# Fused attention and two MLPs in float32: GpSimd's operations in pieces of 128 columns, one-column thresholds, second PSUM banks for h and y, the low parts of k on VectorE

## The chip, the core and the metric

The kernel runs on one core of one Trainium2 chip. The core has a matrix engine (TensorE, PE in the profile), a vector engine (VectorE, DVE), an engine for activation functions (ScalarE, ACT), a programmable engine (GpSimd, POOL in the profile and "Pool" in the kernel) and SyncE (SP), on whose queue all the large DMAs are issued. TensorE writes only to PSUM, a small memory of eight banks per partition; GpSimd works only from SBUF to SBUF. The metric is the device time of one execution in microseconds.

## The reference

All data are float32. A thresholded attention (4 batches, 8 heads, 576 positions, head size 64) feeds an MLP of 512 -> 2048 -> 512 with a SiLU gate, and this a second MLP of 512 -> 1536 -> 512 whose two branches are multiplied.

```
scores = scale * q @ k.T                                  # scale = 1/8
thresh = max(scores) - tau                                # tau = 0.02
scores = where(scores >= thresh, scores, -1e9)
attn = exp(scores - max(scores)); attn /= sum(attn) + 1e-9
x = (attn @ v) as [2304, 512]
h = x @ w_in;  y = (h * sigmoid(h)) @ w_out               # 512 -> 2048 -> 512
a = y @ w_a;  b = y @ w_b;  out = (a * b) @ w_o           # 512 -> 1536 -> 512
```

## The kernel before

A matrix product in float32 is made of three faster products: each operand is split into a high part, rounded to the format fp32r, and a low part, which is the float32 value minus the high one (hi x lo, hi x hi and lo x hi). So every weight, every x, every gated h, every y and z is split by ScalarE (the cast to the high part) and DVE or Pool (the subtraction).

The weights come as pairs of 32-bit words. A block of 128x512 weights passes through `split_weight`: DMA into `wraw`; ScalarE scales the low words (`low`, into `wt`) and the high words (`scale`, into `wc`); DVE masks the sign (`sign`, L323) and joins it to the scaled words (`join`, L328); Pool adds the two (`total`, L332, 128x512); ScalarE casts the high part (`hi`, L336, into `w`); Pool, for some of the second MLP's blocks DVE, subtracts for the low part (`lo`, L340, 128x512). There is one buffer for `wc`, so the next block's `scale` waits for this block's `total`. The first MLP has 32 such blocks, the second 36.

The attention works on 144 tiles of 128 rows by 576 columns. For each, TensorE writes scores to the two-bank PSUM tile `sa` (in the first sixteen tiles, the early ones, in turn `sa` and `sb`); DVE scales them into `t` and finds the lowest (L489); a tiny DVE instruction on 128x1 makes the threshold `thr` (L495 early, L497 later); ScalarE takes the exponential `e` (L503); DVE masks it and sums it (L506, one SBUF input and PSUM in the early tiles, later the two SBUF tensors `t` and `e`); TensorE transposes `e` into `tp`, ScalarE copies that out, and TensorE multiplies with `v`. The sums get 1e-9 added on DVE (`guard`, L435), are inverted, go through DRAM (`r_d`) and come back broadcast as `xi`, Pool multiplies with them (`divide`, L618), and x goes to DRAM as `xT_d`. From tile 54 on q and k are split as well (`split_head`): a cast on ScalarE and two subtractions on Pool (`lo_k`, L402, and `lo_q`, L405, 576 columns each).

The first MLP takes blocks of 256 tokens (j, nine of them) and slices of 128 of the 2048 hidden columns (f, sixteen); a pair (j, f) is a unit, numbered n from 0 to 143. A unit's `mlp1_up` is 12 matmuls into the PSUM bank `hb`; then ScalarE takes the tanh, DVE the gate (`th`, L711, which reads `hb` a last time and so frees it), ScalarE the high part `gh` and DVE the low part `gl` (L717). `mlp1_down` is 12 matmuls into the two-bank tile `sb`, which gathers y over the sixteen units of a token block and is then copied out in two halves by ScalarE and DVE (`yo`, L765); y goes through DRAM (`yT_d`) to the second MLP, whose units write the PSUM pair `ps_a` and `ps_b` (two pairs in turn, opened when attention closes).

The order of instructions on every engine is written ahead of time by a planner, the class `Plan`: each task has an engine, a cost in ns, a rank and the tasks that it waits for; the planner runs through time, gives each idle engine its ready task of lowest rank, and records the program in that order. At run time each engine keeps its order and waits on semaphores. While the attention has gaps on TensorE, units of the first MLP fill them, and in the longest gaps transposes of `ident` into `tp` that nobody reads (filler). A number of the planner concerns us: tasks of DVE and Pool that are marked `port` cannot run at the same time, so whichever comes second is given the remaining time of the other on top:

```
shared = max(0, min(port["Pool" if e == "DVE" else "DVE"] - now, t["cost"]))
port[e] = end = done = end + self.SHARED * shared
```

Of the kernel before, what the change touches and what calls it, by code (L numbers as in the profile page):

```python
# [21 lines left out]
P = 128  # L22
# [38 lines left out]
class Plan:  # L61
# [15 lines left out]

    SHARED = 1.0
# [42 lines left out]
    def run(self):  # L121
# [4 lines left out]
        port = {"DVE": 0, "Pool": 0}  # L126
# [12 lines left out]
        while events:  # L139
# [13 lines left out]
            for e, q in ready.items():  # L153
                if idle[e] and q:
# [41 lines left out]
def pool_ns(n):  # L196
    return int(2.35 * n + 90)
# [7 lines left out]
def fused_kernel(ctx: ExitStack, tc: tile.TileContext, qk, qk2, v, tau, w_in, w_out, w_a, w_b, w_o2, out):  # L205
# [25 lines left out]
    RINGS = dict(qk=2, sp=2, v=1, t=2, e=4, pa=1, pb=1, sa=1, sb=1, tp=2, hb=1, av=1, x=1, xi=1, rs=1,  # L231
# [48 lines left out]

    back = const.tile([P, 1], F32, name="back")
# [16 lines left out]
    def split_weight(key, src, rank, dst, after=(), lo_engine="Pool", scale_engine="DVE"):  # L298
# [32 lines left out]
        def total():  # L331
            nc.gpsimd.tensor_tensor(out=s["t"], in0=s["c"].bitcast(U32), in1=s["t"], op=ALU.add)  # L332
# [5 lines left out]
        def lo():  # L338
            eng = nc.gpsimd if lo_engine == "Pool" else nc.vector
            eng.tensor_tensor(out=wt[key][:, 1, :], in0=s["t"].bitcast(F32), in1=wt[key][:, 0, :].bitcast(F32),  # L340
                              op=ALU.subtract)
# [48 lines left out]
    def split_head(n, b, h):  # L390
# [18 lines left out]
        q, k = (add("Pool", pool_ns(S), n + R_SPLIT, f, [up]) for f in (lo_q, lo_k))  # L409
# [17 lines left out]
    def inverses(n, m):  # L427
# [6 lines left out]
        def guard():  # L434
            nc.vector.tensor_scalar(out=s["sum"][:, :m], in0=s["sum"][:, :m], scalar1=EPS, scalar2=None, op0=ALU.add)  # L435
# [19 lines left out]
    def softmax(parts, total):  # L455
# [69 lines left out]
    def weigh(b, half, c, tiles, v, last):  # L525
# [91 lines left out]
        def divide():  # L617
            nc.gpsimd.tensor_tensor(out=s["x"][:, :nq], in0=s["x"][:, :nq], in1=s["i"][:, :nq], op=ALU.mult)  # L618
# [40 lines left out]
    def load_x(j):  # L659
        s = xs[j] = {}  # L660

        def split(c):
# [12 lines left out]
            def lo():  # L675
                nc.gpsimd.tensor_tensor(out=s["l", c], in0=s["r", c], in1=s["h", c].bitcast(F32), op=ALU.subtract)
# [13 lines left out]

# [305 lines left out]
```

## Time and profile before

| what | us |
|---|---|
| median of 3 runs (1200.87 to 1204.55) | 1202.97 |
| the profiled execution | 1202.49 |
| its span | 1200.7 |
| TensorE busy (97% of the span) | 1162.6 |
| weight loads busy (83%) | 998.2 |
| DVE busy (54%) | 648.1 |
| ScalarE busy (45%) | 544.5 |
| Pool busy (23%) | 278.9 |

The span is from the first to the last instruction of the program, and the profiled execution's own time is 1.8 us more. An engine's busy time is the time in which at least one of its instructions runs; a time spent waiting inside an instruction counts as busy. Matmuls follow each other more closely than they last, so TensorE's busy time is no measure of its work; the number of matmuls in a stretch says more.

### The profile page before, as it was taken

What the parts mean: (1) busy time and instruction counts of PE and PEld (TensorE: products, weight loads), DVE (VectorE), ACT (ScalarE), POOL (GpSimd) and SP (SyncE); (2) the same over time, 40 slices, a digit from 0 to 9 for tenths busy, and PEclk for the clock granted to TensorE, in tenths of its full rate; (3) what the DMA queues carried; (4) which work ended last, traced back from release to release, by engine and by line L of the source; (5) the groups of instructions that cost most, each with busy time, mean ns of one, the idle gap of its engine ahead of it and who ended that gap; (6) DMA issues with size and microseconds to landing.
All of it is one profiled execution on the core that took longest, in us unless ns stands there. A gap on an engine that the chain in (4) does not pass through costs nothing.

```text
span 1200.7 us, 19670 instructions
## 1 busy us (share of the span) xinstructions
PE 1162.6 (97%) x7675; PEld 998.2 (83%) x7675; DVE 648.1 (54%) x1428; ACT 544.5 (45%) x1071; POOL 278.9 (23%) x232
## 2 busy tenths in 40 slices
PE   8889989999999999989999999999999999999998
PEld 5556667888888888889999999888888888888898
DVE  7989898777777777473233258765311211221121
ACT  7777777666666666443233245443211211211121
POOL 3656554233322322130000024443000000000000
PEclk9989999999999999999999999999999999999999
DMA  5655543222322220351010023432200200000000
GB/s 190 195 176 150 160 152 129 80 85 86 97 72 71 89 89 32 101 166 36 1 37 27 1 66 117 152 123 71 70 1 1 70 1 1 18 36 1 1 36 18
DMA packets 43276, 90.14 MB, mean 75 GB/s; under 512 B 4384, under 2 KB 22448, under 8 KB 43184
## 3 DMA queue, kind: packets, MB, share of 16 engines
q1 hardware_dynamic: 43040, 88.89, 23.0%
q8 instruction: 60, 0.98, 0.4%
q14 instruction: 32, 0.26, 0.1%
q10 hardware_dynamic: 144, 0.00, 0.0%
HBM read 74.65 MB, written 14.23 MB: 74 GB/s over the span
## 4 chain that ended last, share of the span: by engine, by line
PE 76%; DVE 10%; DMA 5%; issue 4%; ACT 4%; POOL 1%; SPq 0%; DVEq 0%; ACTq 0%; POOLq 0%
PE op L869 12%; PE ps_b L825 12%; PE ps_a L825 12%; PE hb L699 12%; PE sb L746 12%; PE av L583 5%; PE tp L538 5%; PE sa L473 4%; DVE e L506 3%; DMA xi<-r_d 2%; DVE t L489 1%; DVE wraw L323 1%; DVE thr L497 1%; DVE wc L328 1%; DVE gl L717 1%
## 5 line engine op out<-in xcount | busy, mean ns | idle before, releaser
L699 PE MATMUL hb<-xh,w 128*128 128x256 f32 x1152 | 225.1, 290 | 6.0 <-DVE th L711 3.9
L699 PEld LDWEIGHTS hb<-xh,w 128*128 128x128 f32 x1152 | 179.3, 192 | 14.2 <-DVE th L711 6.2
L746 PE MATMUL sb<-gh,w 128*128 128x256 f32 x1152 | 169.6, 286 | 2.3 <-DVE yo L765 1.8
L699 PE MATMUL hb<-xl,w 128*128 128x256 f32 x576 | 162.9, 283 | 0.0
L835 DVE TENSOR_TENSOR z<-ps_b,z 128x512 f32<-128x512 f32 (+1 forms) x60 | 38.2, 636 | 230.2 <-PE ps_b L825 230.2
L746 PEld LDWEIGHTS sb<-gh,w 128*128 128x128 f32 x1152 | 150.5, 192 | 6.6 <-DVE yo L765 2.8
L506 DVE SCALAR_TENSOR_TENSOR e<-t,thr,e 128x576 f32<-128x576 f32 x128 | 129.7, 1014 | 21.8 <-ACT e L503 20.8
L825 PE MATMUL ps_a<-yh,w 128*128 128x512 f32 (+1 forms) x480 | 137.0, 370 | 0.0
L825 PE MATMUL ps_b<-yh,w 128*128 128x512 f32 (+1 forms) x480 | 136.6, 369 | 0.0
L869 PE MATMUL op<-w,zh 128*128 128x512 f32 x432 | 134.3, 392 | 0.0
L489 DVE TENSOR_SCALAR_CACHE_REDUCE t<-sa,nscale 128x576 f32<-128x576 f32 x128 | 103.6, 809 | 51.6 <-PE sa L473 49.6
L538 PE MATMUL tp<-ident,e 128*128 128x128 f32 x706 | 106.5, 280 | 13.9 <-DVE e L506 10.0
L711 DVE SCALAR_TENSOR_TENSOR th<-th,hb 128x256 f32<-128x256 f32 x144 | 60.2, 418 | 107.2 <-ACT th L708 106.8
L332 POOL TENSOR_TENSOR wt<-wc,wt 128x512 uint32<-128x512 uint32 x68 | 91.2, 1342 | 109.5 <-DVE wc L328 91.3
L503 ACT ACTIVATE e<-t,min 128x576 f32<-128x576 f32 x128 | 99.6, 780 | 28.2 <-DVE t L489 27.5
L708 ACT ACTIVATE th<-hb 128x256 f32<-128x256 f32 x144 | 55.0, 382 | 122.3 <-PE hb L699 113.2
L699 PEld LDWEIGHTS hb<-xl,w 128*128 128x128 f32 x576 | 110.1, 191 | 0.0
L538 PEld LDWEIGHTS tp<-ident,e 128*128 128x128 f32 x706 | 78.8, 141 | 37.4 <-DVE e L506 16.7
L832 ACT COPY z<-ps_a 128x512 f32<-128x512 f32 (+1 forms) x60 | 32.5, 542 | 162.5 <-PE ps_a L825 162.4
L825 PEld LDWEIGHTS ps_a<-yh,w 128*128 128x128 f32 x480 | 87.5, 188 | 16.7
L825 PEld LDWEIGHTS ps_b<-yh,w 128*128 128x128 f32 x480 | 86.8, 188 | 15.4
L717 DVE TENSOR_TENSOR gl<-th,gh 128x256 fp32r<-128x256 f32 x144 | 76.0, 528 | 36.8 <-ACT gh L714 36.4
(85 smaller groups left out, 1901.9 us busy)
## 6 DMA issues: line engine op xcount, KB each, us to landing
qk<-qk SPq DMA_DIRECT2D x20, 576.0 KB
wraw<-w_in SPq DMA_DIRECT2D x16, 512.0 KB
wraw<-w_out SPq DMA_DIRECT2D x16, 512.0 KB
v<-v SPq DMA_DIRECT2D x20, 320.0 KB
wraw<-w_a SPq DMA_DIRECT2D x12, 512.0 KB
wraw<-w_b SPq DMA_DIRECT2D x12, 512.0 KB
wraw<-w_o SPq DMA_DIRECT2D x12, 512.0 KB
xr<-xT_d SPq DMA_DIRECT2D x36, 128.0 KB
```

The lines of the kernel that those rows point to most:

```text
L332: nc.gpsimd.tensor_tensor(out=s["t"], in0=s["c"].bitcast(U32), in1=s["t"], op=ALU.add)
L489: nc.vector.tensor_scalar(out=s["t"], in0=s["s"][:, :, :NH], scalar1=nscale, scalar2=None, op0=ALU.mult, op1=ALU.min, accum_out=s["min"])
L503: nc.scalar.activation(out=s["e"], in_=s["t"], func=AF.Exp, scale=-1.0, bias=s["min"])
L506: nc.vector.scalar_tensor_tensor(out=s["e"], in0=s["s"][:, :, :NH] if early else s["t"], scalar=s["thr"], in1=s["e"], op0=ALU.is_ge if ear ...
L538: nc.tensor.transpose(t["tp"][:, j * P:(j + 1) * P], e["e"][:, o:o + P], ident)
L583: nc.tensor.matmul(s["av"][h * D:(h + 1) * D, :nq], lhsT=v["v"][:, h, k], rhs=s["p"][:, k, h * nq:(h + 1) * nq], start=(k == 0), stop=(k = ...
L699: nc.tensor.matmul(s["h"], lhsT=w[:, a, o:o + P], rhs=xx, start=(c == 0 and k == 0), stop=(c == NC - 1 and k == 2))
L711: nc.vector.scalar_tensor_tensor(out=s["t"], in0=s["t"], scalar=1.0, in1=s["h"], op0=ALU.add, op1=ALU.mult)
L717: nc.vector.tensor_sub(out=s["gl"], in0=s["t"], in1=s["gh"].bitcast(F32))
L746: nc.tensor.matmul(ys[j][:, e, :], lhsT=w[:, a, e * P:(e + 1) * P], rhs=gs[j, f][g], start=(f == 0 and e % 2 == 0 and a == 1), stop=(f == ...
L825: nc.tensor.matmul(s[nm][:, :tn], lhsT=w[:, a, o:o + P], rhs=yy[:, :tn], start=(c == 0 and k == 0), stop=(c == NC - 1 and k == 2))
L869: nc.tensor.matmul(o_ps[t0, i], lhsT=s[z][:, i * P:(i + 1) * P], rhs=wt["o2", f][:, a, :], start=(f == 0 and k == 0), stop=(f == NF2 - 1 a ...
```

## The change

- Pool's operations (`total`, `lo`, `divide`, `lo_q` and the low part of x) are issued in pieces of at most 128 columns, one instruction each: four for 512 columns, two for 256, three for 320, five for 576. `pool_ns` counts 90 ns for each piece.
- The planner's lock of the two engines is written anew: a DVE task that comes while Pool is at work waits at most for the end of a piece; a Pool task waits for the whole rest of the DVE task.
- The threshold has one column of scalars: early, -1/SCALE is a constant and `tsub` the column; later, a `tensor_scalar` with the column `tadd` takes the place of the sum of two tensors. The guard of the sums takes its 1e-9 from a column `eps`.
- The low parts of k are made by DVE in one instruction instead of by Pool.
- From unit 64 on, odd units write h to a second bank `hc`, and token blocks 4, 6 and 8 gather y in a second tile `sd`. Both are opened when attention closes. In exchange only one pair `ps_a`, `ps_b` is opened then; the second pair, for the odd units of the second MLP, is opened when the first MLP closes.

```diff
+TWO_H = 64
+PIECE = 128
...
-                        shared = max(0, min(port["Pool" if e == "DVE" else "DVE"] - now, t["cost"]))
-                        port[e] = end = done = end + self.SHARED * shared
+                        other, piece = port["Pool" if e == "DVE" else "DVE"]
+                        end = done = end + (max(0, other - now) % piece if e == "DVE" else max(0, other - now))
+                        port[e] = end, pool_ns(PIECE)
...
 def pool_ns(n):
-    return int(2.35 * n + 90)
+    return int(2.35 * n + 90 * len(pieces(n)))
+def pieces(n):
+    k = -(-n // PIECE)
+    return [slice(n * i // k, n * (i + 1) // k) for i in range(k)]
...
         def total():
-            nc.gpsimd.tensor_tensor(out=s["t"], in0=s["c"].bitcast(U32), in1=s["t"], op=ALU.add)
+            for o in pieces(512):
+                nc.gpsimd.tensor_tensor(out=s["t"][:, o], in0=s["c"][:, o].bitcast(U32), in1=s["t"][:, o], op=ALU.add)
...
         def lo_k():
-            nc.gpsimd.tensor_tensor(out=s["t"][:, 2], in0=s["r"][:, S:], in1=s["t"][:, 1].bitcast(F32), op=ALU.subtract)
+            nc.vector.tensor_tensor(out=s["t"][:, 2], in0=s["r"][:, S:], in1=s["t"][:, 1].bitcast(F32), op=ALU.subtract)
...
-            nc.vector.tensor_scalar(out=s["sum"][:, :m], in0=s["sum"][:, :m], scalar1=EPS, scalar2=None, op0=ALU.add)
+            nc.vector.tensor_scalar(out=s["sum"][:, :m], in0=s["sum"][:, :m], scalar1=eps, scalar2=None, op0=ALU.add)
...
-                nc.vector.tensor_scalar(out=s["thr"], in0=s["min"], scalar1=back, scalar2=tsub, op0=ALU.mult, op1=ALU.add)
+                nc.vector.tensor_scalar(out=s["thr"], in0=s["min"], scalar1=-1 / SCALE, scalar2=tsub, op0=ALU.mult, op1=ALU.add)
             else:
-                nc.vector.tensor_add(out=s["thr"], in0=s["min"], in1=tadd)
+                nc.vector.tensor_scalar(out=s["thr"], in0=s["min"], scalar1=tadd, scalar2=None, op0=ALU.add)
...
+        bank = "hc" if n >= TWO_H and n % 2 else "hb"
...
-                    s["h"] = ps_1.tile([P, 512], F32, name="hb")[:, :TB]
+                    s["h"] = (pools["hc"] if bank == "hc" else ps_1).tile([P, 512], F32, name=bank)[:, :TB]
...
+        ring = "sd" if j * NF >= TWO_H and j % 2 == 0 else "sb"
...
+        pools["hc"] = pool(p1, "ps_hc", 1, space=PSUM)
+        pools["ab", 0] = pool(ctx, "ps_ab", 1, "right", space=PSUM)
...
+        pools["ab", 1] = pool(ctx, "ps_ab2", 1, space=PSUM)
```

Since the planner's costs change, it writes a new order for every engine. On Pool, some 53 us into the program, a weight block's sum `wt`, an attention output `x`, a weight's low part `w` and the low part of x stood like this:

```order
L332 TENSOR_TENSOR wt<-wc,wt 128x512
L618 TENSOR_TENSOR x<-x,xi 128x256
L340 TENSOR_TENSOR w<-wt,w 128x512
L332 TENSOR_TENSOR wt<-wc,wt 128x512
L340 TENSOR_TENSOR w<-wt,w 128x512
L676 TENSOR_TENSOR xl<-xr,xh 128x256
```

The same place on Pool in the changed program:

```order
L344 TENSOR_TENSOR wt<-wc,wt 128x128 x4
L634 TENSOR_TENSOR x<-x,xi 128x128 x2
L353 TENSOR_TENSOR w<-wt,w 128x128 x4
L344 TENSOR_TENSOR wt<-wc,wt 128x128 x4
L353 TENSOR_TENSOR w<-wt,w 128x128 x4
L693 TENSOR_TENSOR xl<-xr,xh 128x128 x2
```

The operations stand in the same sequence; each is two or four instructions.

On DVE, just behind the sixteen early tiles, the lowest score (L489, new L504), the threshold, the mask (L506, new L521), the sign (L323, new L334) and the join of a weight block stood so:

```order
L489 TENSOR_SCALAR t,min<-sa,nscale 128x576
L497 TENSOR_TENSOR thr<-min,tadd 128x1
L489 TENSOR_SCALAR t,min<-sa,nscale 128x576
L506 SCALAR_TENSOR_TENSOR e,sum<-t,thr,e 128x576
L323 TENSOR_SCALAR wraw<-wraw 128x512
L497 TENSOR_TENSOR thr<-min,tadd 128x1
L328 SCALAR_TENSOR_TENSOR wc<-wc,wraw 128x512
```

In the changed program, at the same tiles:

```order
L512 TENSOR_SCALAR thr<-min,tadd 128x1
L521 SCALAR_TENSOR_TENSOR e,sum<-t,thr,e 128x576
L504 TENSOR_SCALAR t,min<-sa,nscale 128x576
L512 TENSOR_SCALAR thr<-min,tadd 128x1
L334 TENSOR_SCALAR wraw<-wraw 128x512
L521 SCALAR_TENSOR_TENSOR e,sum<-t,thr,e 128x576
L339 SCALAR_TENSOR_TENSOR wc<-wc,wraw 128x512
```

The mask of a tile now stands ahead of the next tile's lowest score, and the threshold is another kind of instruction.

On TensorE, after the attention, the end of one unit's `up`, the `down` of the unit before it (`gh`, then `gl`) and the start of the next `up` stood so throughout:

```order
L699 MATMUL hb<-xl,w 128x256
L746 MATMUL sb<-gh,w 128x256 x8
L746 MATMUL sb<-gl,w 128x256 x4
L699 MATMUL hb<-xh,w 128x256 x2
L699 MATMUL hb<-xl,w 128x256
```

In the changed program the end of unit 65's `up`, the `down` of unit 64, which opens token block 4, and the start of unit 66 read:

```order
L718 MATMUL hc<-xl,w 128x256
L768 MATMUL sd<-gh,w 128x256 x8
L768 MATMUL sd<-gl,w 128x256 x4
L718 MATMUL hb<-xh,w 128x256 x2
L718 MATMUL hb<-xl,w 128x256
```

The sequence is the same and the banks take turns. In all the changed program has 64 filler transposes where there were 81 (L536).

## Rows read from the trace of the kernel before

**Rows 1.** Busy time by stage (windows); after the span: PE, PEld, DVE, ACT, POOL.

```profile
0.00:75.00 75.00, 61.69 (x400) 39.36 (x400) 64.07 (x155) 56.88 (x102) 39.72 (x39) 0.95 0.58 188
75.00:200.00 125.00, 116.40 (x856) 87.18 (x855) 114.31 (x250) 96.17 (x191) 69.75 (x55) 1.00 0.49 153
200.00:490.00 290.00, 284.07 (x2279) 251.41 (x2279) 217.37 (x573) 190.05 (x366) 83.69 (x69) 1.00 0.24 78
490.00:530.00 40.00, 35.60 (x278) 34.00 (x275) 23.25 (x44) 19.02 (x43) 12.43 (x11) 0.96 0.51 160
752.00:1200.00 448.00, 444.87 (x2078) 369.49 (x2076) 133.93 (x212) 103.28 (x182) 40.33 (x30) 1.00 0.12 39
```

**Rows 2.** Timeline of DVE from 144 us: start, duration, instruction.

```profile
143.94 0.15 DVE L497 TENSOR_TENSOR thr<-min,tadd 128x1 f32<-128x1 f32 x1
144.01 0.42 DVE L323 TENSOR_SCALAR wraw<-wraw 128x512 uint32<-128x512 uint32 x1
144.34 0.81 DVE L506 SCALAR_TENSOR_TENSOR e<-t,thr,e 128x576 f32<-128x576 f32 x1
...
145.08 0.68 DVE L328 SCALAR_TENSOR_TENSOR wc<-wc,wraw 128x512 uint32<-128x512 uint32 x1
...
147.80 0.44 DVE L717 TENSOR_TENSOR gl<-th,gh 128x256 fp32r<-128x256 f32 x1
```

**Rows 3.** DVE's groups, 0 to 75 us: count, busy us, mean ns, idle before.

```profile
L323 DVE TENSOR_SCALAR wraw<-wraw 128x512 uint32<-128x512 uint32 x13 | 11.3, 872 | 1.4 <-ACT wc L317 1.0
...
L497 DVE TENSOR_TENSOR thr<-min,tadd 128x1 f32<-128x1 f32 x6 | 2.6, 437 | 0.1
L435 DVE TENSOR_SCALAR sum<-sum 128x4 f32<-128x4 f32 x4 | 2.3, 574 | 0.0
```

**Rows 4.** DVE's groups, 75 to 200 us.

```profile
L506 DVE SCALAR_TENSOR_TENSOR e<-t,thr,e 128x576 f32<-128x576 f32 x32 | 32.5, 1015 | 4.1 <-ACT e L503 3.9
...
L323 DVE TENSOR_SCALAR wraw<-wraw 128x512 uint32<-128x512 uint32 x19 | 17.3, 912 | 2.6 <-ACT wc L317 2.6
...
L497 DVE TENSOR_TENSOR thr<-min,tadd 128x1 f32<-128x1 f32 x33 | 13.2, 401 | 0.2
L717 DVE TENSOR_TENSOR gl<-th,gh 128x256 fp32r<-128x256 f32 x17 | 10.2, 598 | 0.7 <-ACT gh L714 0.6
```

**Rows 5.** DVE's groups, 200 to 490 us.

```profile
L506 DVE SCALAR_TENSOR_TENSOR e<-t,thr,e 128x576 f32<-128x576 f32 x90 | 91.4, 1016 | 16.5 <-ACT e L503 15.8 <-DVE sum L435 0.3
...
L717 DVE TENSOR_TENSOR gl<-th,gh 128x256 fp32r<-128x256 f32 x42 | 26.0, 620 | 0.9 <-ACT gh L714 0.9
L497 DVE TENSOR_TENSOR thr<-min,tadd 128x1 f32<-128x1 f32 x89 | 20.5, 230 | 1.3
```

**Rows 6.** Timeline of all engines, 50 to 52 us; here Pool and DVE.

```profile
50.13 1.29 POOL L340 TENSOR_TENSOR w<-wt,w 128x512 fp32r<-128x512 f32 x1 [0.96 <-ACT w L336]
...
50.72 0.99 DVE L323 TENSOR_SCALAR wraw<-wraw 128x512 uint32<-128x512 uint32 x1
...
51.38 0.92 POOL L676 TENSOR_TENSOR xl<-xr,xh 128x256 fp32r<-128x256 f32 x1
51.63 0.69 DVE L435 TENSOR_SCALAR sum<-sum 128x4 f32<-128x4 f32 x1
```

**Rows 7.** Timeline of Pool from 37 us.

```profile
37.45 0.72 POOL L676 TENSOR_TENSOR xl<-xr,xh 128x256 fp32r<-128x256 f32 x1 [1.71 <-ACT xh L673]
38.14 1.26 POOL L332 TENSOR_TENSOR wt<-wc,wt 128x512 uint32<-128x512 uint32 x1
```

**Rows 8.** Timeline of DVE at 5 us.

```profile
5.12 0.21 DVE L284 TENSOR_SCALAR tsub<-tadd,back 128x1 f32<-128x1 f32 x1
```

**Rows 9.** Pool's groups, 75 to 200 us.

```profile
L340 POOL TENSOR_TENSOR w<-wt,w 128x512 fp32r<-128x512 f32 x20 | 27.8, 1392 | 19.5 <-ACT w L336 19.5
```

**Rows 10.** Waits from 490 to 752 us: total, times, longest.

```profile
PEld hb L699 <- DVE th L711: 6.0, 9, 1.7
...
PEld sb L746 <- DVE yo L765: 2.8, 5, 2.0
```

More of the change, by code (lines that the diff above doesn't have):

```diff
@@ L76 @@
     WINDOW = 3413
-    SHARED = 1.0
     def __init__(self):
@@ L125, in run @@
         pipe, window, cold, spans = 0, 0, False, [(0, 4400)]
-        port = {"DVE": 0, "Pool": 0}
+        port = {"DVE": (0, 1), "Pool": (0, 1)}
         free = 0
@@ L338, in lo @@
         def lo():
-            eng = nc.gpsimd if lo_engine == "Pool" else nc.vector
-            eng.tensor_tensor(out=wt[key][:, 1, :], in0=s["t"].bitcast(F32), in1=wt[key][:, 0, :].bitcast(F32),
-                              op=ALU.subtract)
+            eng, parts = (nc.gpsimd, pieces(512)) if lo_engine == "Pool" else (nc.vector, [slice(0, 512)])
+            for o in parts:
+                eng.tensor_tensor(out=wt[key][:, 1, o], in0=s["t"][:, o].bitcast(F32), in1=wt[key][:, 0, o].bitcast(F32),
+                                  op=ALU.subtract)
         a = dma(rank, P * 4096, load, take=["wraw"], behind=after)
@@ L617, in divide @@
         def divide():
-            nc.gpsimd.tensor_tensor(out=s["x"][:, :nq], in0=s["x"][:, :nq], in1=s["i"][:, :nq], op=ALU.mult)
+            for o in pieces(nq):
+                nc.gpsimd.tensor_tensor(out=s["x"][:, o], in0=s["x"][:, o], in1=s["i"][:, o], op=ALU.mult)
         def store():
@@ L675, in lo @@
             def lo():
-                nc.gpsimd.tensor_tensor(out=s["l", c], in0=s["r", c], in1=s["h", c].bitcast(F32), op=ALU.subtract)
+                for o in pieces(TB):
+                    nc.gpsimd.tensor_tensor(out=s["l", c][:, o], in0=s["r", c][:, o], in1=s["h", c][:, o].bitcast(F32), op=ALU.subtract)
             ld = dma(-1, P * 4 * TB, load, after=need, take=["xr"], slack=SLACK)
@@ L721, in mlp1_up @@
             p = pl.add("PE", 3 * pe_ns(TB), R, up(c),
-                       [*x_ready[j, c], *w_ready["in", c, f // 4]], ["hb"] if c == 0 else [], behind=[up_last[0]])
+                       [*x_ready[j, c], *w_ready["in", c, f // 4]], [bank] if c == 0 else [],
+                       behind=[up_last[0], *([closed] if c == 0 and bank == "hc" else [])])
             up_last[0] = p
@@ L753, in mlp1_down @@
             p = pl.add("PE", 4 * pe_ns(TB), R, down(k0), [g_ready[j, f][k0 == 8], *w_ready["out", f]],
-                       ["sb"] if f == 0 and k0 == 0 else [], behind=[down_last[0]])
+                       [ring] if f == 0 and k0 == 0 else [], behind=[down_last[0]])
             down_last[0] = p
@@ L907, in fused_kernel, with close_attention @@
             pair(b, c, (0, 1))
+    def close_attention():
+        att.close()
+        right.close()
+        open_transit()
+        pools["w2"] = pool(ctx, "wpool2", RINGS["w2"], "right")
+        pools["y"] = pool(ctx, "yb", 6, "right")
+        pools["hc"] = pool(p1, "ps_hc", 1, space=PSUM)
+        pools["ab", 0] = pool(ctx, "ps_ab", 1, "right", space=PSUM)
+    closed = pl.add("none", 1, 0, close_attention, behind=[*att_tasks, *closed0])
     units = [(j, f) for j in range(NB) for f in range(NF)]
```

28 lines of the change are left out of this document (12 added, 16 removed).

## The prediction

> **What bounds the kernel now.** I read the page's span first, then the busy time by stage, then each engine's instructions stage by stage, then single instructions in order of time. The profiled execution took 1202.49 us, 1200.7 of it span and 1.8 around it; the median of the runs shown is 1202.97, so I reckon from 1202.5.
>
> By stage [rows 1] TensorE is busy for 444.87 of the 448 us from 752 on: there only fewer matmuls would help, and none is removed. From 200 to 490 it is busy for 284.07 of 290. It waits at the start (13.3 us idle in the first 75), from 75 to 200 (8.6 us), and from 490 to 530 (4.4 us). Idle time understates this, because a matmul's row lasts longer than its turn: from 75 to 200 TensorE issues 856 matmuls in 125 us, 6.85 per us, from 200 to 490 it issues 7.86. At the later rate the 856 would take 109 us, so this stage has about 16 us to give. The engine that is nearly full there is VectorE (DVE), with 64.07 of 75 and 114.31 of 125 us.
>
> Part of that DVE time is waiting inside instructions. Undisturbed, the steps take 0.15 us (threshold, L497), 0.42 (sign, L323), 0.81 (mask, L506), 0.68 (join, L328) and 0.44 (low part of the gate, L717) [rows 2]; most stage means are far above [rows 3 to 5]. The reason can be seen at 50.7 us [rows 6]: L323 starts while Pool's L340 (50.13 to 51.42) is at work, takes 0.99 instead of 0.42 and ends at 51.71, 0.29 after Pool's end. Both engines read SBUF through something that only one can have. The excess over the undisturbed time, count by (mean minus undisturbed):
> 0 to 75: L323 13 x 0.45 = 5.9, L497 6 x 0.29 = 1.7, L435 4 x 0.42 = 1.7 (taking 0.15 for an undisturbed one), together 9.3 us.
> 75 to 200: L506 32 x 0.205 = 6.6, L323 19 x 0.49 = 9.3, L497 33 x 0.25 = 8.3, L717 17 x 0.16 = 2.7, together 26.9 us.
> 200 to 490: L506 90 x 0.206 = 18.5, L717 42 x 0.18 = 7.6, L497 89 x 0.08 = 7.1, together 33.2 us.
>
> **The pieces.** They help only if a waiting DVE instruction gets in between two Pool instructions that follow each other at once. It does [rows 6]: Pool's L676 was queued behind L340 and began at 51.38, L323 still ended at 51.71, and L676 took 0.92 us, against 0.72 for an undisturbed one [rows 7]. So a handover costs Pool about 0.2 us here.
>
> What a piece costs: two Pool instructions in a row start 0.69 us apart when the first has 256 columns [rows 7] and 1.25 us apart with 512 [rows 6]. That is 2.19 ns a column and 0.13 us fixed, so a piece of 128 takes 0.41, four take 1.64 instead of 1.25. A DVE instruction that comes at any moment waits half of what stands before it, 0.62 us before and 0.21 after, a third; Pool is at work 1.31 times as long, so it is met 1.31 times as often. What is left of such a wait is 0.33 x 1.31 = 0.44.
>
> **The thresholds.** A threshold with two SBUF tensors waits for Pool; the new form has one tensor and a column of scalars. The nearest row is L284, that very form and size, at 0.21 us [rows 8]; against the 0.15 of L497 that is 0.06 more for each of 128, and I take the wait as gone (bounds: gone, or 0.44 of it left, 3.6 us in the first 200). The sixteen early thresholds lose one of two columns, even at 0.1 us each 1.6 us in all, taken as nothing. The guard of the sums (L435, 128x4) gets a column in place of a constant; no row shows whether that frees it, so of its 1.7 us nothing or 0.44 of it, 0.7, is left; I take 0.4. By the Trainium skill (SBUF — State Buffer, Who interferes with whom, with the condition in VectorE: DVE Perf Modes, Mode 2×_2P) a one-tensor instruction from SBUF to SBUF takes the shared pair of ports when its outermost dimension is even, or odd and equal on both sides, whatever its scalars are. By that the guard would go on waiting and the sum would be 0.3 us higher; no run here shows it.
>
> DVE's saving. First 75 us: 9.3 − 0.44 x 5.9 − 6 x 0.06 − 0.4 (guard) = 5.9. 75 to 200: 26.9 − 0.44 x 18.6 − 33 x 0.06 = 16.7.
>
> 200 to 490: 33.2 − 0.44 x 26.1 − 89 x 0.06 = 16.4, from which go the 20 low parts of k that DVE now does. I price these as the undisturbed mask, also 576 columns, 0.74 us from the start of one at 144.34 to the next instruction at 145.08 [rows 2], 14.8 us. That leaves 1.6 on an engine that has 73 us idle there, while TensorE lacks 6.
>
> **What that is worth.** In the first 75 us DVE's saving goes on to the first MLP work only where DVE, not a DMA or ScalarE, ends the wait: 4 of 5.9 (bounds 0 and 5.9). From 75 to 200 I take half of 16.7, 8 (bounds 0 and the 16 that TensorE has to give), because order and pace also depend on ScalarE (96.17 of 125 busy) and on Pool. From 200 to 490: 1.
>
> **What Pool pays.** It is busy 39.72 + 69.75 = 109.5 of the first 200 us. Some 65 instructions of 512 columns take 0.39 more, 25 us; about 119 DVE instructions there can hold it up (32 signs, as many joins, 17 gates, some 38 masks), and if half meet it at 0.2 each, 12 more. That makes 147 of 200, so Pool does not become the bound, and it has waits to absorb this: before L340 alone it idles 19.5 us from 75 to 200, waiting for ScalarE's cast [rows 9]. But each weight block goes twice through Pool and is some 1.2 us later, and what stands behind the waiting cast on ScalarE (exponentials, copies out of PSUM) is later with it. The plan, which counts 1563 ns for four pieces, allows for most, not for handovers. I charge 4 us (bounds 0 and the whole 37).
>
> **The second banks.** Between 490 and 752 TensorE's weight loads wait 6.0 us for the gate that frees hb and 2.8 for the copy that frees sb, up to 2.0 at once [rows 10]. From 490 to 530 the granted clock is 0.96 of full speed [rows 1], that is 1.6 us lost. Together 10.4. In the new order odd units from 65 on write hc, and the y of the fifth token block goes to sd, so TensorE is one unit (24 matmuls) ahead of the gate. The wait ahead of unit 64 stays (up to 1.7 us), and DVE, which has the second MLP's weights there too, stays behind at times: I take 7 (bounds 3 and 10.4). The second MLP gives up its second ab pair until the first MLP closes, but unit 0's own 24 matmuls cover the two copies that this waits for; nothing.
>
> **Sum:** 1202.5 − 4 − 8 − 1 + 4 − 7 = **1186.5 us**.
>
> **Rivals.**
> *Pool becomes the pace (slower).* If handovers cost more than 0.2 us, Pool fills up: its idle 53 us and the 12 charged are gone when each of the 119 costs 0.55 us. Then the weights arrive at Pool's pace; 37 us of new Pool time against 22.6 saved on DVE makes the first 200 us 14.4 longer, less 8 from the rest: 1209. For it: Pool's two steps per weight block stand in series with ScalarE's and DVE's, all in order. Against it: Pool's idle time [rows 9].
>
> *Only the banks pay.* The plan puts matmuls where it expects gaps; if they are misplaced, TensorE waits as long as before until 490. 1202.5 − 8 = 1194.5.
>
> *The pieces close up.* If pieces of one operation leave no opening, DVE waits 1.31 times as long: 24.5 x 0.31 = 7.6 us more in the first 200, against 9 from thresholds and guard, and Pool's lateness of 4 stays: 1202.5 − 7 + 4 = 1199.5, no change. The Trainium skill (GPSIMD Engine Reference, Instruction dispatch) says that nothing holds the next Pool instruction back until all cores are done with the last, which would speak for this. The handover at 51.4 us [rows 6] speaks against it. No change also comes about if DVE's backlog after 500 moves the saved waits on to the gates: about 1202.
>
> *All of it pays.* 5.9 + 16 + 1 + 10.4 with nothing lost on Pool: 1169.2. Against: two engines would have to follow exactly.
>
> **How the numbers follow.** Two runs of this kernel differ by up to 0.3% (1200.87 to 1204.55), so 3.6 us is what can be told from nothing. Chances: forecast 0.43 (its own range 1178 to 1193), all of it 0.12, only the banks 0.18, no change by either way 0.10, Pool's pace 0.17. Faster 0.73, same 0.10, slower 0.17. Between 1169 and 1204 lie the forecast, the banks alone and no change (0.71), half of the all-of-it case and what of Pool's pace ends before 1204: 0.80.
>
> **What would show it.** L506, L323 and L717 from 75 to 200 should have means of about 0.90, 0.64 and 0.51; L512 about 0.21 with none above 0.3; Pool's pieces 0.41 apart where nothing comes between. After 500 no wait of hc, and at most one longer wait of hb, and a clock of 1.00 past 513. The stage that ends at 200 should be some 8 us shorter with the same work done. I am wrong if ScalarE's casts wait for Pool by more than 4 us in the first 200, if Pool's share there passes 0.9, or if the clock falls in the first 75 us for longer than now (0.95), since the new order has 64 filler transposes instead of 81.

## The result, and the profile after

The changed kernel takes **1213.74 us** (median of 4 runs, 1211.73 to 1214.04), the kernel before 1203.60 (4 runs of the same comparison): a ratio of 1.0084, 95% interval 1.0064 to 1.0105. It is 10 us slower where 16 us less was forecast; the time lies outside the range. The profiled execution has a span of 1211.8 us.

Below, a difference of ratios is turned into us with 1203.6, and a kernel is always compared by its ratio to the kernel before on the same chip.

The busy time by stage of the changed kernel, to be read against [rows 1] (each figure: busy us and instructions; behind the engines the granted clock, DMA share, GB/s):

```profile
core 0: us, PE busy (x) PEld busy (x) DVE busy (x) ACT busy (x) POOL busy (x), PEclk, DMA share, GB/s
0.00:75.00 75.00, 63.53 (x407) 40.48 (x408) 57.10 (x158) 56.18 (x100) 51.29 (x108) 0.93 0.57 181
75.00:200.00 125.00, 113.29 (x795) 82.64 (x794) 97.39 (x240) 92.79 (x187) 105.69 (x193) 0.97 0.50 152
200.00:490.00 290.00, 286.12 (x2300) 255.62 (x2299) 215.84 (x599) 191.72 (x371) 104.18 (x179) 0.99 0.25 81
490.00:530.00 40.00, 36.81 (x296) 35.62 (x296) 24.02 (x48) 18.77 (x44) 18.46 (x35) 1.00 0.53 167
530.00:752.00 222.00, 219.93 (x1800) 217.42 (x1799) 87.91 (x193) 78.74 (x189) 45.15 (x92) 1.00 0.15 45
752.00:1200.00 448.00, 441.78 (x2020) 361.19 (x2020) 126.90 (x209) 102.09 (x179) 58.06 (x125) 1.00 0.12 38
```

Three things are to be seen. From 75 to 200 DVE is down to 97 us, as meant, but Pool is up to 106 and TensorE issues 795 matmuls, 61 fewer than before [rows 1]. From 490 to 530 the granted clock is 1.00, and more is issued. And past 752, where TensorE had hardly a gap, it now has gaps of 6 us together.

The loss lies behind the first MLP. The first matmul of the second MLP, in the kernel before and in the changed kernel:

```profile
747.26 0.63 PE L825 MATMUL ps_a<-yh,w 128*128 128x512 f32 x2
```

```profile
745.65 0.62 PE L847 MATMUL ps_a<-yh,w 128*128 128x512 f32 x2
```

Up to there the changed kernel is 1.6 us ahead, where the forecast had 16. The time by which it is slower than the kernel before, it loses behind this point.

DVE's groups from 75 to 200, answering [rows 4] (instructions, then busy us and mean ns of one, then idle time before them):

```profile
L521 DVE SCALAR_TENSOR_TENSOR e<-t,thr,e 128x576 f32<-128x576 f32 x31 | 28.9, 935 | 2.8 <-ACT e L518 2.3
L334 DVE TENSOR_SCALAR wraw<-wraw 128x512 uint32<-128x512 uint32 x20 | 11.6, 582 | 15.0 <-ACT wc L328 14.8
L736 DVE TENSOR_TENSOR gl<-th,gh 128x256 fp32r<-128x256 f32 x15 | 8.2, 549 | 2.5 <-ACT gh L733 2.3
L512 DVE TENSOR_SCALAR thr<-min,tadd 128x1 f32<-128x1 f32 x31 | 6.3, 204 | 0.1
```

The means fell to where the prediction put them: mask 0.94 (forecast 0.90), sign 0.58 (0.64), low part of the gate 0.55 (0.51), threshold 0.20 (0.21). With the prediction's counts these four save 16.2 us, of 16.7 forecast. What the change does to DVE is understood; what that is worth isn't. DVE now idles 14.8 us before the signs alone, for ScalarE. And ScalarE, from 0 to 200, waits for Pool:

```profile
ACT w L348 <- POOL wt L344: 15.7, 16, 3.2
ACT wt L323 <- POOL w L353: 14.3, 17, 2.1
```

(us in total, times, longest). In the kernel before, in the same 200 us, the first of them is

```profile
ACT w L336 <- POOL wt L332: 4.4, 5, 1.6
```

and the second isn't among the seven longest waits. The prediction named the casts' wait for Pool as what would make it wrong, from 4 us on. As a sign that was badly set, since the kernel before has 4.4 us of it already; what tells is the growth to 15.7.

Between 490 and 752 the weight loads' waits, answering [rows 10]:

```profile
PEld sd L768 <- ACT gh L733: 4.6, 9, 1.1
PEld hb L718 <- DVE th L730: 3.2, 3, 1.8
PEld sd L768 <- DVE gl L736: 0.4, 1, 0.4
```

There is no wait for hc, as said, but the down step now waits 4.6 us for ScalarE's cast of the gate, where it was 0.9 before.

In the second MLP, where before no weight load waited for a weight, TensorE now catches up with the splitting of the weights (waits of 800 to 835 us):

```profile
PEld ps_a L847 <- POOL w L353: 3.1, 2, 1.6
PEld op L891 <- ACT zh L860: 2.4, 1, 2.4
PEld ps_b L847 <- DVE w L353: 2.3, 1, 2.3
```

### The profile page after: what moved, and what is told of

Read it like the earlier page. It is cut to its first block, busy times and chain, and to the rows that moved or that the text cites. A ratio compares the mean times of both kernels' runs of the same rounds, so it can differ in the third digit from the quotient of the medians.

```text
span 1211.8 us, 20246 instructions
## 1 busy us (share of the span) xinstructions
PE 1169.5 (97%) x7658; PEld 999.8 (83%) x7658; DVE 611.6 (50%) x1449; ACT 542.2 (45%) x1071; POOL 382.8 (32%) x730
## 5 line engine op out<-in xcount | busy, mean ns | idle before, releaser
L718 PE MATMUL hb<-xh,w 128*128 128x256 f32 x832 | 166.6, 294 | 6.2 <-DVE th L730 4.3
L344 POOL TENSOR_TENSOR wt<-wc,wt 128x128 uint32<-128x128 uint32 x272 | 128.6, 503 | 75.6 <-DVE wc L339 51.2
L718 PEld LDWEIGHTS hb<-xh,w 128*128 128x128 f32 x832 | 130.4, 193 | 12.8 <-DVE th L730 5.3
L353 POOL TENSOR_TENSOR w<-wt,w 128x128 fp32r<-128x128 f32 x200 | 113.6, 598 | 80.3 <-ACT w L348 79.6
L504 DVE TENSOR_SCALAR_CACHE_REDUCE t<-sa,nscale 128x576 f32<-128x576 f32 x128 | 103.5, 809 | 45.3 <-PE sa L488 39.0
L521 DVE SCALAR_TENSOR_TENSOR e<-t,thr,e 128x576 f32<-128x576 f32 x128 | 113.1, 884 | 19.7 <-ACT e L518 18.1
L718 PE MATMUL hb<-xl,w 128*128 128x256 f32 x416 | 118.6, 285 | 4.1 <-POOL xl L693 4.1
L768 PE MATMUL sb<-gh,w 128*128 128x256 f32 x768 | 115.6, 287 | 1.4 <-POOL w L353 1.3
L768 PEld LDWEIGHTS sb<-gh,w 128*128 128x128 f32 x768 | 101.1, 191 | 3.3 <-POOL w L353 2.2
L891 PEld LDWEIGHTS op<-w,zh 128*128 128x128 f32 x432 | 80.9, 189 | 19.7 <-ACT zh L860 2.4
L860 ACT CAST zh<-z 128x512 fp32r<-128x512 f32 (+1 forms) x60 | 34.5, 576 | 124.4 <-DVE z L857 124.4
```

Source lines behind the costliest of these rows:

```text
L344: nc.gpsimd.tensor_tensor(out=s["t"][:, o], in0=s["c"][:, o].bitcast(U32), in1=s["t"][:, o], op=ALU.add)
L353: eng.tensor_tensor(out=wt[key][:, 1, o], in0=s["t"][:, o].bitcast(F32), in1=wt[key][:, 0, o].bitcast(F32), op=ALU.subtract)
L504: nc.vector.tensor_scalar(out=s["t"], in0=s["s"][:, :, :NH], scalar1=nscale, scalar2=None, op0=ALU.mult, op1=ALU.min, accum_out=s["min"])
L521: nc.vector.scalar_tensor_tensor(out=s["e"], in0=s["s"][:, :, :NH] if early else s["t"], scalar=s["thr"], in1=s["e"], op0=ALU.is_ge if ear ...
L718: nc.tensor.matmul(s["h"], lhsT=w[:, a, o:o + P], rhs=xx, start=(c == 0 and k == 0), stop=(c == NC - 1 and k == 2))
L768: nc.tensor.matmul(ys[j][:, e, :], lhsT=w[:, a, e * P:(e + 1) * P], rhs=gs[j, f][g], start=(f == 0 and e % 2 == 0 and a == 1), stop=(f == ...
```

## The experiments

Two theories to begin with. **Pieces:** four instructions in place of one make each of Pool's steps longer, and the weight blocks come later, in the second MLP above all. **Banks:** giving up the second pair of a and b banks costs the second MLP its time. Against both, **order:** the new plan puts things in a poorer order, whatever each takes.

### 1. Late whole operations, all whole, banks alone, banks undone

whole_late: the changed kernel, order unchanged, whole Pool operations in the second MLP. whole: everywhere.

```
-            for o in pieces(512):
+            for o in pieces(512) if rank < 1e6 else [slice(0, 512)]:
```

> The changed kernel, same order of all instructions, but the two Pool steps of the second MLP's 36 weight blocks are one instruction of 512 columns each again (the first MLP's stay in pieces). Theory 'pieces': in the second MLP each block is about 0.4 us later at each Pool step and a DVE instruction let in between holds Pool another 0.5 us, so TensorE catches up with the blocks at 812 to 828 us; whole operations take those gaps away, 7.4 us and the 1.7 us of half clock behind them: about 1205 us (1203 to 1207), gaps at 812 to 828 below 1 us in all. Rival 'banks': the second pair of a and b banks, which comes only when the first MLP closes, is what makes the second MLP longer: no change from 1213.7 (1212 to 1215). Rival 'order': the new order of instructions puts the blocks too late, whatever each takes: 1211 to 1214.

> The changed kernel, same order of all instructions, but every Pool operation is one instruction again, in the attention too. Theory 'pieces': the second MLP as in the kernel with late whole operations (1205), and in the first 200 us Pool's 86 us of time held up by let-in DVE instructions is gone while DVE's waits come back; the changed kernel is 4.3 us behind there, so 1201 to 1205. Rival 'order': 1211 to 1214, as the order is the changed one. If the pieces do pay in the first 200 us (as the prediction had it), this one is slower than the one with late whole operations, by up to 8 us: 1205 to 1213.

banks_only: the kernel before with TWO_H, hc, sd and the split ab pools of the diff and no more. one_bank: the changed kernel with these undone.

> The kernel before with the second banks for h and y (and the second a and b pair that comes when the first MLP closes) and nothing else of the change. Theory 'pieces': the banks gain what the changed kernel shows between 490 and 752 us, 3.6 us, and the 1.7 us of half clock at 514: 1197.5 to 1200. Rival 'banks': the second MLP is longer with them: 1205 or more, with the loss past 752 us, and matmuls into ps_a and ps_b 233 ns apart instead of 230.

> The changed kernel without the second banks: one h bank, one y pair, both a and b pairs from the end of the attention on, as before. Theory 'pieces': what the banks gain is given up, 1216 to 1219, and the gaps at 812 to 828 us stay. Rival 'banks': the second MLP loses its 13 us again: 1204 to 1207, with matmuls into ps_a and ps_b 230 ns apart.

Measured: whole_late 1202.07 us, ratio 0.9983 [0.9969, 0.9997]; whole 1203.50, 0.9991 [0.9979, 1.0002]; banks_only 1198.41, 0.9946 [0.9928, 0.9963]; one_bank 1213.51, 1.0082 [1.0063, 1.0101].

So late pieces alone cost 12 us (1.0084 - 0.9983), shown with every instruction in its place. Pool in the changed kernel (start and duration of a run of equal instructions, idle time before it):

```profile
811.34 1.70 POOL L344 TENSOR_TENSOR wt<-wc,wt 128x128 uint32<-128x128 uint32 x4 [2.70 <-ACT z L854]
813.77 2.20 POOL L353 TENSOR_TENSOR w<-wt,w 128x128 fp32r<-128x128 f32 x4 [0.73 <-ACT w L348]
...
822.75 2.21 POOL L353 TENSOR_TENSOR w<-wt,w 128x128 fp32r<-128x128 f32 x4 [0.73 <-ACT w L348]
```

and in whole_late:

```profile
805.64 1.34 POOL L353 TENSOR_TENSOR w<-wt,w 128x512 fp32r<-128x512 f32 x1 [0.74 <-ACT w L348]
...
811.66 1.29 POOL L344 TENSOR_TENSOR wt<-wc,wt 128x512 uint32<-128x512 uint32 x1 [2.75 <-DVE wc L339]
813.68 1.34 POOL L353 TENSOR_TENSOR w<-wt,w 128x512 fp32r<-128x512 f32 x1 [0.73 <-ACT w L348]
```

Four pieces alone take 1.70 instead of 1.29. With a DVE instruction let in they take 2.20 instead of 1.34. It is the join of the next block, and the second piece is the one that it holds up:

```profile
814.00 0.82 DVE L339 SCALAR_TENSOR_TENSOR wc<-wc,wraw 128x512 uint32<-128x512 uint32 x1
814.24 0.90 POOL L353 TENSOR_TENSOR w<-wt,w 128x128 fp32r<-128x128 f32 x1
```

It cost Pool 0.5 us. Every second low part is Pool's, so from one to the next is a pair of blocks: 8.98 us against 8.04. The low part at 822.75 us is the same one as that at 813.68 in whole_late. Seven pairs earlier the two stood at 759.52 and 757.33, so over these seven the lateness grows from 2.2 to 9.1 us; before that, from 710 us on, a pair takes 9 to 10 us in either kernel. TensorE has no lead to take this up. Even in whole_late its weight loads just reach the weights (waits of 752 to 1200 us):

```profile
PEld ps_b L847 <- DVE w L353: 0.8, 1, 0.8
PEld ps_a L847 <- POOL w L353: 0.7, 1, 0.7
```

So nearly all of the 9.1 us is passed on: the two profiled spans differ by 9.7. A part of it is clock: from 800 to 835 us, where TensorE stands, the granted clock is 0.95 in the changed kernel and 1.00 in whole_late, and 113 matmuls are issued instead of 147. The groups of 752 to 870 us show how it is passed on, first in the changed kernel, then in whole_late:

```profile
L348 ACT CAST w<-wt 128x512 fp32r<-128x512 f32 x21 | 13.1, 623 | 27.3 <-POOL wt L344 27.2
L330 DVE TENSOR_SCALAR wc<-wraw 128x512 f32<-128x512 f32 x20 | 8.5, 423 | 25.0 <-POOL wt L344 25.0
```

```profile
L348 ACT CAST w<-wt 128x512 fp32r<-128x512 f32 x21 | 13.1, 624 | 13.5 <-POOL wt L344 13.1
L330 DVE TENSOR_SCALAR wc<-wraw 128x512 f32<-128x512 f32 x20 | 8.5, 425 | 17.8 <-POOL wt L344 17.8
```

There is one buffer wc, so DVE's first step of the next block waits for Pool's total of this one, as ScalarE's cast does: the steps of a block stand in series, and Pool's time is in the series. This path is read from the waits; a second buffer wc was not run.

The banks alone gain 6.5 us. In the changed kernel taking them away changes nothing (1.0082 against 1.0084, a miss for all that was expected). The gain is missing there before the second MLP begins: its first matmul starts at 744.75 us in one_bank and at 745.65 with the banks. From 490 to 752 the weight loads of one_bank wait 9.6 us in all:

```profile
PEld hb L718 <- DVE th L730: 7.3, 8, 1.4
PEld sb L768 <- DVE yo L787: 1.2, 5, 0.5
PEld sb L768 <- ACT gh L733: 1.1, 1, 1.1
```

With the banks it is 8.2 (the rows above), over half of it for the cast of the gate instead; banks_only brings these waits from 10.2 to 5.0. Why they stay in the changed kernel isn't settled. The banks theory falls. That whole and whole_late stand level says that in this order the pieces of the attention neither gain nor lose.

### 2. The column, and the thresholds

In the changed kernel matmuls into ps_a and ps_b take some 3 ns more, of which nothing so far gave the reason; banks_only doesn't show it. The one new tile in SBUF is eps.

no_eps: the changed kernel without it. late_no_eps: whole_late without it. banks_pad: banks_only with an unused column in its place. banks_thr: banks_only with the thresholds of the diff.

```
-    eps = const.tile([P, 1], F32, name="eps")
-    nc.vector.memset(eps, EPS)
...
-            nc.vector.tensor_scalar(out=s["sum"][:, :m], in0=s["sum"][:, :m], scalar1=eps, ...
+            nc.vector.tensor_scalar(out=s["sum"][:, :m], in0=s["sum"][:, :m], scalar1=EPS, ...
```

> The changed kernel without the column eps (four bytes a partition, allocated ahead of nearly all other tiles); the guard of the sums adds a constant again, and nothing else differs. In the changed kernel matmuls into ps_a and ps_b start 233 to 234 ns apart, in the kernel with the second banks alone 228 to 232, as before; over some 1,700 of them that is 4 to 5 us. Theory 'place': the new column moves all tiles behind it in SBUF, and the weights and values of the second MLP are read a little slower from where they lie now: 1208.5 to 1210, matmuls at 230 ns. Rival: the pace has another cause (the pieces, the order): 1213 to 1214.5, matmuls at 233 to 234 ns.

> The kernel before with the second banks alone, and one unused column of four bytes a partition where the changed kernel allocates eps. It computes nothing that is used. Theory 'place': 4 to 5 us slower than without the column (1198.4): 1202.5 to 1203.5, matmuls into ps_a and ps_b 233 to 234 ns apart. Rival: no change, 1198 to 1199, 230 ns.

> The changed kernel with whole Pool operations in the second MLP and without the column eps. Both losses undone: 1202.1 - 4.5 = 1197.5 (1196.5 to 1198.5) by theory 'place'; 1202 if the column does nothing. Against the second banks alone (1198.4) it holds the pieces in the attention, the new lock in the plan, the one-column thresholds and k's low parts on DVE: if the saved waits of DVE were worth what the prediction took (9 us net until 490), 1189; if they are worth nothing, within 1.5 us of 1198.4.

> The kernel before with the second banks and the one-column thresholds (no pieces, no column eps). By the prediction the thresholds' waits, 8.3 us of DVE's time from 75 to 200 and 7.1 from 200 to 490, are gone, half of the first worth 4 us: 1194. Theory that DVE's saved waits don't reach the end, because the first MLP's matmuls wait for something else there: within 1.5 us of 1198.4.

Measured: no_eps 1212.29, 1.0064 [1.0048, 1.0080]; banks_pad 1201.74, 0.9978 [0.9966, 0.9990]; late_no_eps 1201.92, 0.9982 [0.9971, 0.9993]; banks_thr 1192.26, 0.9906 [0.9887, 0.9925].

The column does set the pace of these matmuls: mean 392 ns in banks_only, 395 in banks_pad (rows below), and in no_eps and late_no_eps the means are again 392. It isn't the chip: banks_thr, on the same chip as banks_pad, has 392. On banks_only the column costs 3.9 us. But in the changed order nothing came back for late_no_eps (0.9983 to 0.9982) and 2.4 us, about half of what was expected and with overlapping intervals, for no_eps; both come to the end of the first MLP some 2 us later than their twins, and why isn't settled. The guard itself takes 213 to 512 ns with the column (median 225) and 152 to 423 with the constant (median 164): the column frees nothing there. By the rule of the Trainium skill (SBUF — State Buffer, Who interferes with whom), which the prediction weighed, the guard would go on waiting. The trace agrees: one of the longest, 0.50 us at 139.50, lies within a run of Pool's pieces (138.58 to 140.38).

The thresholds alone are worth 4.8 us beyond the banks, near the 4.4 of their expectation (1198.4 to 1194): what they save DVE does reach the end.

### 3. Which part of the rest loses: order, pieces, k's low parts, the lock

late_no_eps is 9 us slower than banks_thr; between them lie the plan, the pieces of the attention and k's low parts. Each was put alone on banks_thr. bt_plan: the changed plan's costs and lock, whole operations (k's low parts stay on Pool, so the order is near the changed one and not the same). bt_pieces: order kept, pieces of 128 until the end of the attention. bt_lok: k's low parts on DVE, old plan. bt_lock: as bt_plan with PIECE = 1024, so that only the lock rule is new (and the down step that takes sd first is put behind the end of the attention too).

> The kernel with second banks and one-column thresholds (1192.3), its operations all whole, but put in order by the changed kernel's plan: Pool's operations costed as pieces (1563 ns for 512 columns instead of 1293), and the new rule for the lock. k's low parts stay on Pool. Theory 'order': most of the 9.6 us by which the changed kernel without its late pieces and without the column is slower than 1192.3 is the order that this plan makes: 1198 to 1202. Rival 'pieces': the loss is the pieces at run time: 1191 to 1194.

> The kernel with second banks and one-column thresholds (1192.3), same order of all instructions, but Pool's operations up to the end of the attention in pieces of 128 columns (the second MLP's whole). Theory 'handover': a piece takes 0.41 us instead of a quarter of 1.25, and each DVE instruction let in holds Pool about half a us, so Pool's lateness eats what DVE gains: 1193 to 1197. The prediction's step: DVE's shorter waits are worth 3 us or more net here: 1187 to 1190.

> The kernel with second banks and one-column thresholds (1192.3), with k's low parts on DVE and the order that the old plan makes of that; no pieces. The prediction took this for free (DVE has 73 us idle from 200 to 490): 1191.5 to 1193.5. Rival: the 20 instructions of 0.74 us stand before thresholds and masks in DVE's queue, and TensorE's attention waits for those: 1194 to 1198.

> As the kernel with the changed kernel's plan and whole operations, but the plan's piece size is 1024, so that it costs Pool's operations as whole ones (1293 ns) and only the rule for the lock is new: DVE waits for what is left of Pool's operation, Pool for what is left of DVE's, and neither stretches the other by the shared time. Theory: the costs of the pieces make the poor order, this one is at 1191 to 1194. Rival: the new rule for the lock itself makes it: 1197 to 1202.

Measured: bt_plan 1202.57, 0.9986 [0.9973, 0.9999]; bt_pieces 1203.87, 1.0010 [0.9997, 1.0023]; bt_lok 1191.15, 0.9892 [0.9878, 0.9907]; bt_lock 1199.13, 0.9954 [0.9938, 0.9971].

**The pieces cost 12.5 us in the attention, too, in an order made for whole operations** (1.0010 - 0.9906), where 1 to 5 were expected by the one theory and a gain by the prediction. The order made for pieces loses 9.6 us with whole operations; together with the pieces (late_no_eps) the loss is 9. So the two don't add: either the pieces cost, or the order that makes room for them does. The lock rule, with that one down step moved, makes an order that loses 5.8, as its rival had it. k's low parts on DVE cost nothing, as predicted (0.9892 against 0.9906, with overlapping intervals).

Where bt_pieces loses, in the same order. 75 to 200 us by stage, banks_thr, then bt_pieces:

```profile
75.00:200.00 125.00, 118.38 (x871) 88.14 (x868) 112.56 (x253) 96.92 (x193) 72.67 (x57) 1.00 0.50 150
```

```profile
75.00:200.00 125.00, 112.91 (x797) 81.59 (x795) 96.09 (x232) 90.81 (x182) 103.81 (x195) 0.97 0.47 143
```

and ScalarE's two steps that wait for Pool, 0 to 200, banks_thr, then bt_pieces:

```profile
L314 ACT ACTIVATE wt<-wraw 128x512 uint32<-128x512 uint32 x32 | 21.8, 680 | 13.0 <-DMA wraw<-w_in 4.7 <-POOL w L342 4.5 <-DMA wraw<-w_out 2.3
L338 ACT CAST w<-wt 128x512 fp32r<-128x512 f32 x32 | 19.6, 614 | 5.3 <-POOL wt L334 5.3
```

```profile
L319 ACT ACTIVATE wt<-wraw 128x512 uint32<-128x512 uint32 x32 | 21.8, 682 | 25.6 <-POOL w L349 23.2 <-DMA wraw<-w_in 1.9 <-DMA wraw<-w_out 0.5
L344 ACT CAST w<-wt 128x512 fp32r<-128x512 f32 x32 | 19.8, 620 | 12.7 <-POOL wt L340 12.1
```

From 75 to 200 DVE is busy 16 us less and Pool 31 more; from 0 to 200 ScalarE waits 35 us for Pool instead of 10. TensorE, which needs ScalarE's exponentials and copies, issues 74 matmuls fewer from 75 to 200.

### 4. Which wait, which size, which place

bt_pieces_wt3: bt_pieces with `bufs=3` for wt, order kept. bt_p256: bt_pieces with pieces of 256. banks_pad16: banks_pad with a column of 16 words. bt_lok_wt3: bt_lok with `bufs=3` for wt.

> The kernel with second banks, one-column thresholds and pieces up to the end of the attention (1203.9), same order, with three buffers instead of two for the tile wt. ScalarE's first step of a weight block then waits for Pool's last step three blocks before, not two; from 0 to 200 us ScalarE now idles 24 us on that wait and 12.2 on its casts' wait for Pool's first step. Theory 'ScalarE's queue': over half of the 11.6 us comes back: 1194 to 1198. Rival 'weights late': ScalarE waits for the same Pool work a step later, the casts' wait grows, and less than a quarter comes back: 1201 to 1204.

> The kernel with second banks, one-column thresholds and pieces up to the end of the attention, same order, with pieces of 256 columns instead of 128: 0.13 us more for an operation of 512 columns instead of 0.4, and one opening in it for DVE instead of three. Theory 'Pool's time': the price goes with the added time, a third of the fixed part and a third of the openings, so 1195 to 1198. Rival: one opening is enough for DVE to hold Pool as often: 1200 to 1204. By the prediction's step (DVE's wait is what counts), between 1192.3 and the forecast for 128: it would be below 1192.

> The kernel with the second banks and an unused column, with the column 64 bytes wide a partition instead of 4. Theory 'boundary': the tiles behind it lie as before by 64 bytes, matmuls into ps_a and ps_b are 228 to 232 ns apart again, and the time is that without the column, 1198.4 (1197.5 to 1199.5). Rival 'any move': 1201 to 1203, 233 to 234 ns.

> The fastest kernel so far (second banks, one-column thresholds, k's low parts on DVE, whole operations on Pool: 1191.2), same order, with three buffers for wt. ScalarE's wait for Pool's last step from 0 to 200 us is under 5 us in a kernel with whole operations, so theory 'ScalarE's queue' expects 0.5 to 2 us: 1189 to 1190.7; if the weights are simply late, 1191.2.

Measured: bt_pieces_wt3 1202.42, 0.9990 [0.9976, 1.0003]; bt_p256 1189.58, 0.9881 [0.9860, 0.9903]; banks_pad16 1194.01, 0.9915 [0.9899, 0.9931]; bt_lok_wt3 1190.56, 0.9893 [0.9874, 0.9912].

The third buffer takes the first wait away and the second grows (0 to 200, bt_pieces_wt3):

```profile
L319 ACT ACTIVATE wt<-wraw 128x512 uint32<-128x512 uint32 x32 | 21.8, 681 | 6.3 <-DMA wraw<-w_out 4.0 <-DMA wraw<-w_in 2.0
L344 ACT CAST w<-wt 128x512 fp32r<-128x512 f32 x31 | 19.2, 618 | 22.9 <-POOL wt L340 22.6
```

The two waits fall from 35 to 23 us together, and the time by 2.4 at most (the intervals overlap). So it isn't the one wait: the buffer mainly shifts where ScalarE stands, and Pool's work on a block is left as the pace, as these rows and the next run say. On bt_lok the third buffer gains nothing either.

Pieces of 256 cost nothing and gain perhaps 3 us (the intervals of 0.9881 and 0.9906 overlap). Pool's busy time from 0 to 200 is 111 us with whole operations (38.63 + 72.67), 128 with pieces of 256 (44.13 + 83.65), 155 with 128 (51.38 + 103.81); ScalarE's waits for it in the same order are 10, 18 and 35 us. One opening in an operation of 512 is enough for DVE's signs (0 to 200 us; banks_thr, bt_p256, bt_pieces):

```profile
L325 DVE TENSOR_SCALAR wraw<-wraw 128x512 uint32<-128x512 uint32 x32 | 29.4, 920 | 4.9 <-ACT wc L319 4.6
```

```profile
L330 DVE TENSOR_SCALAR wraw<-wraw 128x512 uint32<-128x512 uint32 x32 | 20.0, 626 | 8.6 <-ACT wc L324 8.2
```

```profile
L330 DVE TENSOR_SCALAR wraw<-wraw 128x512 uint32<-128x512 uint32 x32 | 19.9, 623 | 14.5 <-ACT wc L324 14.2
```

It isn't for the rest: the joins' means are 752, 860 and 766 ns, and over signs, joins, masks and low parts of the gate two pieces save DVE some 5 us where four save 12. But four take 27 us more of Pool's time than two.

The column of 64 bytes was expected to restore the time without a column or to keep the loss. It did neither: 3.7 us faster than without (the two intervals just touch). Matmuls of 870 to 1100 us, mean ns in the next to last figure, of banks_only, banks_pad and banks_pad16:

```profile
L831 PE MATMUL ps_b<-yh,w 128*128 128x512 f32 x224 | 69.5, 392 | 0.0
```

```profile
L833 PE MATMUL ps_b<-yh,w 128*128 128x512 f32 x224 | 70.3, 395 | 0.0
```

```profile
L877 PE MATMUL op<-w,zh 128*128 128x512 f32 x230 | 71.0, 389 | 0.0
L833 PE MATMUL ps_b<-yh,w 128*128 128x512 f32 x224 | 69.0, 389 | 0.0
```

### 5. The change with pieces of 256, and what paid put together

after_p256: the changed kernel with PIECE = 256. best: bt_lok with pieces of 256 in the attention, order kept, and the column of 64 bytes.

> The changed kernel with PIECE at 256 instead of 128, in its plan and in what runs; nothing else. Theory 'size of the piece': in the second MLP a third of the 11.6 us stays (each Pool step 0.13 us longer instead of 0.4), in the attention the loss turns into nothing or a small gain: 1213.7 - 7.7 - 4 to 8 = 1198 to 1202, with the gaps at 812 to 828 us below 3 us. Rival 'any piece is too many': 1206 or more. The kernel still has the column eps, worth 3 us.

> Second banks, one-column thresholds, k's low parts on DVE, the old plan, Pool's operations up to the end of the attention in pieces of 256 (the second MLP's whole) and an unused column of 64 bytes. If the gains add: 1191.2 - 2.7 - 4.4 = 1184 (1182 to 1186). If the pieces of 256 and k's low parts on DVE gain the same waits, 1186 to 1188. Matmuls of the second MLP 227 ns apart.

Measured: after_p256 1206.27, 1.0026 [1.0015, 1.0037], just inside the rival's: 7 us better than with 128, where 12 to 16 were expected, and still slower than before. The waits for weights in the second MLP are not below 3 us together:

```profile
PEld ps_b L847 <- DVE w L353: 2.2, 1, 2.2
PEld ps_a L847 <- POOL w L353: 2.0, 1, 2.0
```

best 1187.39, **0.9866** [0.9846, 0.9886]: 16 us faster than the kernel before; of the gains found one by one (13.0 for bt_lok, 3.7 for the place, 3 for pieces of 256) some 3.5 don't add, as the second of its expectations had it; the reason that it gives wasn't traced.

## Why the prediction was wrong

**The step that failed is the price of the pieces.** "I charge 4 us (bounds 0 and the whole 37)" measured 12.5 net of all that DVE gains from them, in the attention (in the order made for whole operations), and the sum had no term at all for the second MLP, where they cost 12. Pool's time was about right (147 forecast of 200, 155 in bt_pieces, 157 in the changed kernel). Wrong was to read Pool's idle time, 53 us, as slack: Pool's steps stand in series with ScalarE's and DVE's, each in order with other work behind it, so added time is passed on long before Pool is full. The handover looked at was also dearer: a join let in cost Pool 0.5 us, not 0.2 as read at 51 us [rows 6].

**The second MLP** was passed over with "there only fewer matmuls would help" [rows 1]. True for a gain; for a loss the question is how far ahead the producer is, and the page doesn't show that. Each block goes through Pool there too, and TensorE had no lead: it just reached the weights with whole operations, and with pieces they came 9.1 us later.

**DVE's saving** was right in its means and in its sum. What it is worth was half right: with thresholds (4.8) it reaches the end, with pieces it is eaten. **The banks** were right in size, 6.5 against 7, but only in the old order: in the changed kernel they are worth nothing, and why is open. **The guard's column** was credited with 1.3 of the 1.7 us that guards waited in the first 75 us, and it frees nothing; that it moves the tiles behind it, 3.9 us on banks_only, the sum didn't have. **k's low parts** were rightly taken as free.

**Order** was not in the sum. The plan with the new lock and piece costs makes an order that loses 9.6 us with whole operations, and in the changed kernel's own order the attention's pieces no longer lose anything (whole against whole_late). So there the attention's loss is one of order; which places in the order lose wasn't traced.

Of the rivals, *Pool becomes the pace* (1209) had the mechanism, with ScalarE's casts in series as its argument for; its condition, handovers of 0.55 us that fill Pool, wasn't needed: Pool's share from 75 to 200 is 0.83 in bt_pieces and 0.85 in the changed kernel. That its 1209 lies near 1213.74 is partly luck, since it had all of its loss in the first 200 us and none in the second MLP. That the clock falls was said too: 0.93 in the first 75 us.

From the kernel before to the changed one, run by run: banks and thresholds -11.3, the attention's pieces, order and k's low parts +9.1 (late_no_eps against banks_thr), the column in this order 0, late pieces +12.2, together +10 (each step is uncertain by 2 to 3 us). That they add up is no proof, as each run is compared with the one before it; that each step is what it is called rests on the runs.

## What to carry to other kernels

An engine's idle share isn't slack when its steps stand in series with those of in-order engines. Price a longer step by how far its consumers are ahead, stage by stage, in the stages that show no wait too. Cutting an operation so that another engine gets in has a best size; here, in the attention, two pieces were free and four cost 12 us, and four cost 12 again in the second MLP. And a gain measured alone need not hold in another order: the banks gave 6.5 us alone and nothing in the changed kernel.

## What the runs showed of the hardware

The place of tiles in SBUF changes the pace of matmuls of 512 columns. In the programs as built, the unused column of banks_pad moves the weights' first tile from byte 1440 of a partition to 1472, and the column of 64 bytes to 1504; the second MLP's up matmuls have means of 392, 395 and 389 ns, and the kernel's time goes by +3.9 and -3.7 us. It isn't the chip: bt_p256, on the same chip as the 389, has 392. Three places don't make a rule, no reason is known, and the values y stayed where they were. A Pool instruction that lets a DVE instruction in is longer for it: four pieces took 2.20 us with a join of 0.82 let in, 1.70 without.
